# Pairs of inverses moved whole and in place, and one store per segment for rows and left products

## The chip, the cores and the metric

The kernel runs on one core of a Trainium2 chip. The metric is the time of one execution in device microseconds; lower is better. TensorE (PE) multiplies matrices, with weight loads (PEld) beside it; VectorE (DVE), ScalarE (ACT) and GpSimd (POOL) work elementwise; transfers run on 16 DMA engines and are issued from the queues of SP, ACT and POOL. A queue issues in its order: an issue that has to wait holds all behind it.

## What is computed

Two independent halves, laid side by side along the last axis of the output, (1, 2048, 2048) bf16.

```python
def _A_ref(x, mem0, Wq, Wk, Wv, Wo, seg_len):       # x (1, 2048, 1024), 32 heads of 128, seg_len 32
    mem = mem0                                      # (1, 8, 1024)
    for s in range(n_seg):                          # 64 segments, one after the other
        h = jnp.concatenate([mem, xs], axis=1)      # 8 + 32 rows
        q, k, v = (einsum('btd,dhe->bhte', h, W) for W in (Wq, Wk, Wv))
        p = _softmax(where(mask, einsum('bhqe,bhke->bhqk', q, k) * scale, -1e9))
        o = einsum('bhte,hed->btd', einsum('bhqk,bhke->bhqe', p, v), Wo)
        mem = o[:, :M, :].copy()                    # the first 8 rows go on
        outs.append(o[:, M:, :])                    # 32 rows are output

def _B_ref(u, A_re, A_im, B_re, B_im, C_re, C_im, log_dt, Dskip):   # u (1, 2048, 1024)
    K = einsum('dn,dnl,dn->dl', Cc, exp(logdA * l), dB).real
    y = irfft(rfft(u padded) * rfft(K padded))      # a long convolution per channel
    return y + u * Dskip
```

## The kernel before

**Three stages.** First tables are built for the convolution and, in between, everything of the first half that does not depend on the running memory is projected ahead. Of the 40 rows of a segment the last 8 ("left" rows) are such: their keys, queries and values come from DRAM tensors PKd and VXd. Then the transform runs, and then the loop over 64 segments, which ends in one large product for the left rows.

**The transform** (part_b) works in 16 blocks: b // 4 is a quarter of the channels (dq, 256 columns), b % 4 a part of the frequencies. A block multiplies the spectrum of u (read from DRAM by load_u, line 1212) with that of K (pointwise, lines 1377 to 1381 and 1463 on VectorE, L1466 on POOL). While quarter dq is being built, the quarter before it is turned back: two of its eight inverses per block from block 4 on, and the last eight after block 15. An inverse (line 1515) yields 2 x 128 rows of 256 columns: 16 products with MI (L1512), and one with the identity (L1524) that adds u times Dskip; ScalarE scales the sum (L1526) into a tile yb of three buffers, and ACT's queue stores yb one inverse later (L1529). The rows of u come on SP's queue, one transfer of 128 KB per inverse (load_inverse, L1481), three inverses ahead; two neighbours share a tile uu of three buffers, which VectorE multiplies by Dskip (skips, L1489).

SP's queue is written by hand: after these loads, or between them, it issues the segments' weights (load_resident, L268, 512 KB each) as places for them come free. The last eight places are the buffers of MI; they are freed one by one by the last eight inverses, and the weight for each is issued behind the inverse that frees it. K for the second half of the channels is loaded in block 6 (L1095).

**The loop over segments** (part_a). Most weights stay in SBUF. Twelve blocks of 512 KB do not fit and are read again in each segment from DRAM copies WD (stage, L340) into four buffers wst on SP's queue. One block, K7, is held in two PSUM banks and copied in each segment to a scratch area called arena by four copies on VectorE (load_kept and fetch, through words, L335). TensorE's products with them are L414 (q, k, v) and L527 (Wo). The small inputs come on ACT's queue: arena<-PKd (L376), needed first by POOL L428, and arena<-VXd (L382). The segment's result lies in arena as ob: ob[:, 0] holds the 32 rows by 4 quarters of the columns, ob[:, 1] the weighted values of the left rows. Two stores on ACT's queue take them away at the end of the segment:

```python
392:         nc.scalar.dma_start(out=OLd[s // 8][:, 256 * (s % 8):256 * (s % 8) + 256], in_=ob[:, 1, :])
393:         rows = out_a[s * SL:s * SL + SL, :].rearrange("r (q d) -> q r d", q=4)
394:         if s + 1 < NS:
395: 
396:             nc.scalar.dma_start(out=rows, in_=ob[:, 0, :])
```

The next segment writes over ob again with its evicted q (ACT L420) and its softmax (DVE L465), which therefore wait until the stores have landed.

**The end.** In the last segment two of eight pieces of OLd, each of 8 segments, are read back (raw, L576), the other six after it (L652); POOL and VectorE sort them by head (L573); TensorE multiplies them with Wo in four blocks of 64 products (L664), and each block's rows XM to SL of its segments are stored (L670).

The framework puts in all semaphore waits. A transfer also waits until the one eight before it has landed.

Of the kernel before, what the change touches and what calls it, by code (L numbers as in the profile page):

```python
# [10 lines left out]
BF16 = mybir.dt.bfloat16  # L11
# [4 lines left out]
ACT = mybir.ActivationFunctionType  # L16
# [58 lines left out]
class Ahead:  # L75
# [3 lines left out]
    def __init__(self, ctx, tc, x, src, seg_len):  # L79
        self.nc, self.tc, self.x, self.src = tc.nc, tc, x, src  # L80
        self.S, self.Dm = x.shape
        self.SL, self.XM = seg_len, 24
        self.XL, self.KC, self.NS = seg_len - 24, self.Dm // 128, self.S // seg_len
        dram = ctx.enter_context(tc.tile_pool(name="a_dram", bufs=1, space=bass.MemoryType.DRAM))
        self.VXd = dram.tile([self.NS + 1, 128, 256 + self.KC * self.XM], BF16, name="VXd")
        self.PKd = dram.tile([self.NS, 128, 512], BF16, name="PKd")
        self.PVd = [dram.tile([self.NS * self.XL, 2048], BF16, name="PVd%d" % t) for t in range(2)]
        self.OLd = dram.tile([self.NS // 8, 128, 8 * 256], BF16, name="OLd")

    def open(self, ctx):  # L90
        self.pool = ctx.enter_context(self.tc.tile_pool(name="a_pre", bufs=1, side="right"))
# [166 lines left out]


EARLY = (6, 3)  # L260
PAIRS = (0, 4, 2, 6, 8, 12, 10, 14)
LATE = 8


# [7 lines left out]
def part_a(ctx, tc, x, src, WD, HE, seg_len, out_a, ahead, W_res, rest, places, first):  # L272
    nc = tc.nc
    S, Dm = x.shape
    M = 8
    SL = seg_len
    E = 128
    KC = Dm // 128
    NS = S // SL
    assert SL == 32 and M == 8 and Dm == 1024 and HE == 4096  # L280
    XM = 24
# [1 line left out]
    NK = SL + M  # L283
    scale = float(E ** -0.5)

    VXd, PKd, OLd = ahead.VXd, ahead.PKd, ahead.OLd
    ident, mask, BD, BDx, BDL, hT = ahead.consts
    mx, S_ = ahead.low["mx"], ahead.low["S"]

# [53 lines left out]
    def load_kept(key):  # L343
        kept[key] = {}
        for n in (1,) if key in HALF else (0, 1):
            kept[key][n] = ps_k.tile([128, 512], F32, name="keep", tag="keep%d" % sum(len(b) for b in kept.values()))
        if key in HALF:
            w = wst.tile([128, 2048], BF16, name="wst", tag="w%d" % (loads[0] % SLOTS))
            loads[0] += 1
            h_ = ahead.low["half"] if key[0] == "q" else wres.tile([128, 1024], BF16, name="Whalf")  # L350
            for n, t_ in ((1, w[:, 0:1024]), (0, h_[:])):
                nc.sync.dma_start(out=t_, in_=src(key)[:, n, :] if key[0] == "o" else src(key)[:, 1024 * n:1024 * n + 1024])
            words(kept[key][1][:], w[:, 0:1024])
            halves[key] = [(0, 1024, h_)]
# [46 lines left out]
    load_kept(("k", 0, 7))  # L401
    fetch(("k", 0, 7))
    pk = load_pk(0)
    between["q", 0, 2] = lambda: load_kept(("q", 0, 7))
    between["v", 0, 7] = lambda: load_kept(("o", 15))
    for s in range(NS):
        def quads(m, t, kcs, a=None):
            if a is None:
                a = ps.tile([128, 512], F32, name="acc", tag=BANK[m, t])
            for kc in kcs:  # L410
                w = unit((m, t, kc))
                for g in range(4):
                    for o_, rhs in columns(w, 512 * g, 512):
                        nc.tensor.matmul(a[32 * g:32 * g + 32, o_:o_ + rhs.shape[1]], lhsT=hT[:, kc, :], rhs=rhs,  # L414
                                         start=(kc == 0), stop=(kc == KC - 1), tile_position=(0, 32 * g), skip_group_check=True)
            return a

        def evac(a, name):
            q = at(name, 512)
            nc.scalar.copy(out=q, in_=a[:])  # L420
            return q
# [156 lines left out]
        quads("v", 0, range(4, KC), a)  # L578
        scores(1, sc1, QT1, KT1)
# [69 lines left out]
                nc.sync.dma_start(out=wo[u][:].rearrange("e (h d) -> e h d", h=2), in_=src(("o", u)))  # L649
    stores(NS - 1, ob)  # L650
    for j in range(2, 8):
        nc.sync.dma_start(out=raw[j][:], in_=OLd[j])  # L652
# [56 lines left out]
def part_b(ctx, tc, u, A_re, A_im, B_re, B_im, C_re, C_im, log_dt, Dskip, out_b, ahead, copies, residents, first_state):  # L709
# [761 lines left out]
    NIV = 3  # L1471
    unsent, pairs, turn_of = [], [], [0]

    def load_inverse(dq, c):
        r, mc = c // 4, c % 4
        i = turn_of[0] % 2
        turn_of[0] += 1
        if i == 0:
            pairs.append(iv.tile([128, 2, 2, DQ], BF16, name="uu", tag="uu", bufs=3))
        uu = pairs[-1][:, i]  # L1480
        sy.dma_start(out=uu, in_=u_v[r][:, mc:mc + 2, DQ * dq:DQ * dq + DQ])  # L1481
        return uu

    def skips():
        dq = todo[0][0]
        uu = pairs.pop(0)
        d = slice(DQ * dq, DQ * dq + DQ)
        uu = uu[:].rearrange("p i a d -> p (i a) d")
        v.tensor_tensor(out=uu, in0=uu, in1=Dsk[:, d].unsqueeze(1).to_broadcast([128, 4, DQ]), op=ALU.mult)  # L1489

    def inverses(n):

        for _ in range(n):
            dq, c = todo.pop(0)
            inverse(dq, c, nxt.pop(0))
            if len(todo) >= NIV:
                nxt.append(load_inverse(*todo[NIV - 1]))

    early = {}

# [14 lines left out]
    def inverse(dq, c, uu):  # L1515
        r, mc = c // 4, c % 4
        d = slice(DQ * dq, DQ * dq + DQ)
        if (dq, c) in early:
            yp = early[dq, c]
            products_back(yp, dq, c, range(3, 4))  # L1520
        else:
            yp = ps_y.tile([128, 2, DQ], F32, name="yp", tag="yp")[:]
            products_back(yp, dq, c, range(4))
        pe.matmul(yp.rearrange("p b d -> p (b d)"), lhsT=ident[:], rhs=uu.rearrange("p b d -> p (b d)"), start=False, stop=True, skip_group_check=True)  # L1524
        yb = iv.tile([128, 2, DQ], BF16, name="yb", tag="yb", bufs=3)
        sc.activation(out=yb[:], in_=yp, func=ACT.Copy, scale=float(2.0 / PLEN))  # L1526
        while unsent:
            unsent.pop(0)()
        unsent.append(lambda: sc.dma_start(out=out_v[r][:, mc:mc + 2, d], in_=yb[:]))  # L1529

    todo = [(dq, c) for dq in range(4) for c in PAIRS]
    nxt = []
    Bs = [None] * 4
    l4 = k1[0:4, 2560:3072].rearrange("p (r n) -> p r n", r=4)
    w4 = k1[0:4, 3072:4096]
    for b in range(16):
# [3 lines left out]
        points = pointwise(b, now)  # L1540
        next(points)
        if b >= 4:
            skips()
        if 0 < b < 15:
            load_u(b + 1)
        if b == 3:
            v.tensor_scalar(out=ident[:], in0=ident[:], scalar1=float(PLEN / 2), scalar2=None, op0=ALU.mult)
            nxt = [load_inverse(*todo[n_]) for n_ in range(NIV)]
# [41 lines left out]
        if b == 10:  # L1590
            state.send(ps_y.tile([128, 8, 128], BF16, name="yp", tag="yp")[:, :, 0:8])
        if b >= 4:
            inverses(2)
    begun = [ps_h.tile([128, 2, 2, DQ], F32, name="hps", tag="h") for _ in range(2)]
    for n_ in range(3):
        inverse_begin(3, PAIRS[n_], begun[n_ // 2][:, n_ % 2])
    ctx2.close()
    for n_ in range(8):
        if n_ % 2 == 0:
            skips()  # L1600
# [5 lines left out]
    while unsent:  # L1606
        unsent.pop(0)()
    for _ in resident:
        pass

# [157 lines left out]
```

## Time and profile before

| | us |
|---|---|
| median of 3 runs | 1952.72 (1950.53 to 1953.33) |
| the profiled execution | 1947.41 |
| its span | 1945.70 |
| transform's blocks and last inverses, about | 440 to 614 |
| first segment | 614.4 to 648.3 |
| a segment, median of the others | 19.5 |
| left products | 1885.8 to 1941 |

A line of the profile names the line of the code, the engine and the operation, and out<-in by tile names. "PE acc L414 <- DMA wst<-WD_v" is a wait: line 414 on PE could not begin until that transfer landed. In the chain of waits each step is followed back from the end of the program to what released it. A transfer is cut into pieces (packets), each on one of 16 engines; "DMA share" is the busy share of these engines, mean.

### The profile page before, as it was taken

What the parts mean: (1) busy time and instruction counts of PE and PEld (TensorE: products, weight loads), DVE (VectorE), ACT (ScalarE), POOL (GpSimd) and SP (SyncE); (2) the same over time, 40 slices, a digit from 0 to 9 for tenths busy, and PEclk for the clock granted to TensorE, in tenths of its full rate; (3) what the DMA queues carried; (4) which work ended last, traced back from release to release, by engine and by line L of the source; (5) the groups of instructions that cost most, each with busy time, mean ns of one, the idle gap of its engine ahead of it and who ended that gap; (6) DMA issues with size and microseconds to landing.
All of it is one profiled execution on the core that took longest, in us unless ns stands there. A gap on an engine that the chain in (4) does not pass through costs nothing.

```text
span 1945.7 us, 73775 instructions
## 1 busy us (share of the span) xinstructions
PE 1787.6 (92%) x31526; PEld 1092.0 (56%) x31564; DVE 1357.6 (70%) x3362; ACT 918.6 (47%) x1654; POOL 496.5 (26%) x885
## 2 busy tenths in 40 slices
PE   8999999887886899999999999999999999999998
PEld 3666665555763455555555555555555555555554
DVE  8599989888992666666666767666766666666650
ACT  8799989850012344344444444444444443434430
POOL 2354545336552111111111212121112111111130
PEclk9999999878988999999999999999999999999999
DMA  7889898867689999999999999999999999999991
GB/s 216 244 236 273 240 279 240 235 194 248 189 280 306 357 341 354 327 343 343 338 346 351 335 348 348 342 353 339 351 344 340 339 350 336 343 335 338 344 354 32
DMA packets 337341, 591.06 MB, mean 304 GB/s; under 512 B 94848, under 2 KB 211048, under 8 KB 334964
## 3 DMA queue, kind: packets, MB, share of 16 engines
q1 hardware_dynamic: 284824, 531.85, 79.8%
q10 hardware_dynamic: 45532, 29.57, 4.9%
q0 software_dynamic: 6656, 24.92, 3.4%
q8 instruction: 247, 4.05, 0.8%
q14 instruction: 82, 0.67, 0.1%
HBM read 528.78 MB, written 68.47 MB: 307 GB/s over the span
## 4 chain that ended last, share of the span: by engine, by line
PE 45%; DMA 32%; DVE 13%; ACT 6%; issue 3%; POOL 1%; SPq 0%; ACTq 0%; DVEq 0%; POOLq 0%
PE acc L414 20%; DMA wst<-WD_v 11%; DMA wst<-WD_o 9%; PE pp L527 7%; DMA wst<-WD_k 3%; PE pe L664 3%; DMA arena<-PKd 3%; PE tr L425 2%; PE pro L184 2%; DMA out_dram<-arena 2%; PE pro L197 1%; DMA uu<-in_B_u_dram 1%; DVE nr L1266 1%; DMA out_dram<-yb 1%; DMA wst<-WD_q 1%
## 5 line engine op out<-in xcount | busy, mean ns | idle before, releaser
L414 PEld LDWEIGHTS <-a_hT 128*32 128x32 bf16 x12352 | 326.9, 96 | 324.8 <-issue 70.0
L420 ACT CAST arena<-acc 128x512 bf16<-128x512 f32 x384 | 224.7, 585 | 395.0 <-PE acc L414 315.3
L527 PEld LDWEIGHTS <-arena 128*32 128x32 bf16 x8256 | 215.2, 96 | 78.0 <-issue 54.2
L414 PE MATMUL acc<-wst,a_hT 128*32 128x512 bf16 x2304 | 229.7, 382 | 31.4 <-DMA wst<-WD_v 24.1
L428 POOL COPY arena<-arena 128x128 bf16<-128x128 bf16 x128 | 37.4, 292 | 703.7 <-PE tr L425 362.0
L335 DVE TENSOR_SCALAR arena<-keep 128x256 int32<-128x256 int32 (+1 forms) x512 | 175.4, 394 | 28.0 <-PE acc L414 27.9
L414 PE MATMUL acc<-XM,a_hT 128*32 128x512 bf16 x2560 | 173.0, 381 | 0.0
L454 DVE TENSOR_REDUCE a_mx<-sc 128x4 f32<-128x160 f32 (+1 forms) x192 | 71.6, 373 | 79.4 <-PE sc L442 78.0
L197 PE MATMUL pro<-XM,wsl 128*128 128x512 bf16 x480 | 119.5, 387 | 4.7 <-DVE kst L206 1.5
L527 PE MATMUL pp<-W_o,arena 128*32 128x256 bf16 x3584 | 121.5, 273 | 1.4 <-issue 1.4
L414 PE MATMUL acc<-W,a_hT 128*32 128x512 bf16 x1536 | 119.4, 382 | 0.5 <-issue 0.5
L542 DVE COPY arena<-tr 128x512 bf16<-128x512 bf16 x64 | 27.2, 424 | 124.7 <-PE tr L425 124.7
L458 ACT ACTIVATE sc<-sc 128x160 f32<-128x160 f32 (+1 forms) x192 | 63.9, 333 | 104.9 <-DVE sc L455 104.0
L462 DVE TENSOR_REDUCE a_mx<-sc 128x4 f32<-128x160 f32 (+1 forms) x192 | 72.7, 379 | 55.2 <-ACT sc L458 55.0
L489 POOL TENSOR_TENSOR arena<-arena,a_BD 128x128 bf16<-128x128 bf16 x128 | 51.0, 399 | 218.7 <-DVE arena L472 211.5
L1266 DVE TENSOR_SCALAR nr<-ptt 128x456 f32<-128x456 int16 x128 | 80.2, 626 | 31.3 <-PE ptt L1244 28.5
L1258 ACT ACTIVATE E<-pa 128x648 bf16<-128x648 f32 x128 | 87.6, 711 | 17.9 <-PE pa L1250 15.9
L527 PE MATMUL pp<-wst,arena 128*32 128x256 bf16 x1536 | 76.1, 274 | 18.2 <-DMA wst<-WD_o 15.3
L414 PE MATMUL acc<-wq,a_hT 128*32 128x512 bf16 x1024 | 92.5, 383 | 0.0
L425 PEld LDWEIGHTS <-arena 128*128 128x128 bf16 x1024 | 57.9, 98 | 59.6 <-ACT arena L420 28.6
L513 ACT CAST arena<-pv 128x512 bf16<-128x512 f32 (+1 forms) x128 | 61.3, 479 | 63.4 <-PE pv L499 36.4
L414 PE MATMUL acc<-g,a_hT 128*32 128x512 bf16 x1024 | 91.0, 380 | 0.0
(342 smaller groups left out, 3963.2 us busy)
## 6 DMA issues: line engine op xcount, KB each, us to landing
wst<-WD_v SPq DMA_DIRECT2D x256, 512.0 KB
wst<-WD_k SPq DMA_DIRECT2D x192, 512.0 KB
wst<-WD_o SPq DMA_DIRECT2D x192, 512.0 KB
wst<-WD_q SPq DMA_DIRECT2D x128, 512.0 KB
Ud<-ux POOLq DMA_DIRECT2D x16, 1024.0 KB, 7.8
wq<-Ud SPq DMA_DIRECT2D x32, 512.0 KB
wsl<-in_A_Wk_dram SPq DMA_DIRECT2D x16, 512.0 KB
wsl<-in_A_Wv_dram SPq DMA_DIRECT2D x16, 512.0 KB
```

The source lines that it names most:

```text
L197: nc.tensor.matmul(a[:], lhsT=w[:, kc, 128 * j:128 * j + 128], rhs=xTl[:, kc, :, :].rearrange("p s k -> p (s k)"), start=(kc == 0), stop=( ...
L335: nc.vector.tensor_scalar(out=out.bitcast(I32), in0=in_.bitcast(I32), scalar1=0, scalar2=None, op0=ALU.bitwise_or)
L414: nc.tensor.matmul(a[32 * g:32 * g + 32, o_:o_ + rhs.shape[1]], lhsT=hT[:, kc, :], rhs=rhs, start=(kc == 0), stop=(kc == KC - 1), tile_pos ...
L420: nc.scalar.copy(out=q, in_=a[:])
L425: nc.tensor.transpose(out=p[:, hl, :, :].rearrange("p a b -> p (a b)"), in_=q[:, 128 * hl:128 * hl + 128], identity=ident[:])
L454: nc.vector.tensor_reduce(out=m_, in_=x, axis=AX.X, op=ALU.max)
L458: nc.scalar.activation(out=flat(sc, i), in_=flat(sc, i), func=ACT.Exp, scale=scale)
L462: nc.vector.tensor_reduce(out=m_, in_=x, axis=AX.X, op=ALU.add)
L513: copy(out=o[:, i:i + n], in_=p[:, i:i + n, :].rearrange("p a (g q) -> p a g q", g=4))
L527: nc.tensor.matmul(po[32 * qt:32 * qt + 32, o_:o_ + rhs.shape[1]], lhsT=oT[:, h % 4, (h % 16) // 4, :], rhs=rhs, start=False, stop=(h == 3 ...
L1258: sc.activation(out=T["E", r, e // 4][:, lo:lo + 8 * NE].rearrange("p (i c) -> p i c", i=2), in_=T.pop(("p", r, e))[:, :, 0:4 * NE], func= ...
L1266: v.tensor_scalar(out=T["n", r, e // 4][:, lo:lo + 8 * NT], in0=T.pop(("t", r, e))[:, 0:8 * NT].bitcast(I16)[:, 0:16 * NT:2], scalar1=floa ...
```

## The change

- *Pairs.* The inverses are taken in the order 0, 2, 4, ... (PAIRS), so that two neighbours cover the four row groups of one residue r. A pair's rows of u are loaded in one transfer of 256 KB (load_pair), two blocks ahead and in front of that block's weights, and its results are stored in one.
- *In place.* ScalarE writes each result over the rows of u that it used; yb is gone, uu has four buffers, and the last pair has a pool of its own.
- *Order at the end.* The last two pairs are loaded ahead of the seven weights that need no place of MI, and these are issued before the last eight inverses instead of behind the first of them. K is loaded in block 5.
- *First segment.* It reads K7 from the tile it was loaded to; K7 goes to PSUM only after the first k.
- *Loop.* ob is stored whole, 1 KB per partition, to a DRAM tensor RSd. The left products are read back from it in pieces of 512 B (load_raw). The rows of all segments are copied from RSd to the output, DRAM to DRAM, by four transfers on SP's queue after the loop (rows_out).

```diff
-        self.OLd = dram.tile([self.NS // 8, 128, 8 * 256], BF16, name="OLd")
+        self.RSd = dram.tile([self.NS, 128, 512], BF16, name="RSd")
...
-PAIRS = (0, 4, 2, 6, 8, 12, 10, 14)
+PAIRS = (0, 2, 4, 6, 8, 10, 12, 14)
...
     def stores(s, ob):
-        nc.scalar.dma_start(out=OLd[s // 8][:, 256 * (s % 8):256 * (s % 8) + 256], in_=ob[:, 1, :])
-        rows = out_a[s * SL:s * SL + SL, :].rearrange("r (q d) -> q r d", q=4)
-        if s + 1 < NS:
-
-            nc.scalar.dma_start(out=rows, in_=ob[:, 0, :])
-        else:
-            for q in range(4):
-                nc.scalar.dma_start(out=rows[q][0:XM], in_=ob[32 * q:32 * q + XM, 0, :])
-
-    load_kept(("k", 0, 7))
-    fetch(("k", 0, 7))
+        nc.scalar.dma_start(out=RSd[s], in_=ob.rearrange("p a b -> p (a b)"))
+
+    def load_raw(j):
+        nc.sync.dma_start(out=raw[j][:].rearrange("p (s f) -> p s f", s=8), in_=RSd[8 * j:8 * j + 8, :, 256:512].rearrange("s p f -> p s f"))
+
+    def rows_out():
+        rows = out_a.rearrange("(s r) d -> s r d", r=SL)
+        for q in range(4):
+            nc.sync.dma_start(out=rows[:, 0:XM, 256 * q:256 * q + 256], in_=RSd[:, 32 * q:32 * q + XM, 0:256])
+
+    ahead_of["k", 0, 7] = [(0, 2048, first["k", 0, 7])]
...
         k0 = evac(a, "k0")
+        if s == 0:
+            load_kept(("k", 0, 7))
...
     for j in range(2, 8):
-        nc.sync.dma_start(out=raw[j][:], in_=OLd[j])
+        load_raw(j)
+    rows_out()
...
+    def load_pair(n_, pool, bufs=4):
+        uu = held[n_] = pool.tile([128, 2, 2, DQ], BF16, name="uu", tag="uu", bufs=bufs)
+        sy.dma_start(out=uu[:].rearrange("p i a d -> p (i a) d"), in_=rows_of(u_v, n_))
...
+    def inverses(n_, i):
+        while ended:
+            ended.pop(0)()
+        inverse(n_ // 4, PAIRS[2 * n_ % 8 + i], held[n_][:, i])
+        if i:
+            ended.append(lambda: sc.dma_start(out=rows_of(out_v, n_), in_=held[n_][:].rearrange("p i a d -> p (i a) d")))
...
-        yb = iv.tile([128, 2, DQ], BF16, name="yb", tag="yb", bufs=3)
-        sc.activation(out=yb[:], in_=yp, func=ACT.Copy, scale=float(2.0 / PLEN))
...
+        sc.activation(out=uu, in_=yp, func=ACT.Copy, scale=float(2.0 / PLEN))
...
         if 0 < b < 15:
             load_u(b + 1)
+        if b >= 4:
+            load_pair(b - 2, iv)
...
-        if b == 6:
+        if b == 5:
             ks.append(load_k(1, k1[:, 0:2560], 0))
...
     ctx2.close()
+    last = ctx.enter_context(tc.tile_pool(name="b_last", bufs=1))
+    load_pair(14, iv)
+    load_pair(15, last, 1)
+    for _ in range(7):
+        next(resident)
     for n_ in range(8):
         if n_ % 2 == 0:
-            skips()
-        inverses(1)
+            skips(12 + n_ // 2)
+        inverses(12 + n_ // 2, n_ % 2)
         if n_ == 1:
             next(state)
-        for _ in range(9 if n_ == 0 else 1):
-            next(resident, None)
-    while unsent:
-        unsent.pop(0)()
+        next(resident)
+    while ended:
+        ended.pop(0)()
```

More of the change, by code (lines that the diff above doesn't have):

```diff
@@ L284, in part_a @@
     scale = float(E ** -0.5)
-    VXd, PKd, OLd = ahead.VXd, ahead.PKd, ahead.OLd
+    VXd, PKd, RSd = ahead.VXd, ahead.PKd, ahead.RSd
     ident, mask, BD, BDx, BDL, hT = ahead.consts
@@ L651, in part_a @@
     for j in range(2, 8):
-        nc.sync.dma_start(out=raw[j][:], in_=OLd[j])
+        load_raw(j)
+    rows_out()
     for j in range(2, 8):
@@ L1469, in pointwise, with rows_of, skips @@
         eng.tensor_tensor(out=to[:, 2:0:-1], in0=odd[:, 0], in1=odd[:, 1, ::-1], op=ALU.subtract)
[L1471 to L1497, printed above, removed]
+    held, ended = {}, []
+    def rows_of(t_, n_):
+        return t_[n_ % 4][:, :, DQ * (n_ // 4):DQ * (n_ // 4) + DQ]
+    def load_pair(n_, pool, bufs=4):
+        uu = held[n_] = pool.tile([128, 2, 2, DQ], BF16, name="uu", tag="uu", bufs=bufs)
+        sy.dma_start(out=uu[:].rearrange("p i a d -> p (i a) d"), in_=rows_of(u_v, n_))
+    def skips(n_):
+        d = slice(DQ * (n_ // 4), DQ * (n_ // 4) + DQ)
+        uu = held[n_][:].rearrange("p i a d -> p (i a) d")
+        v.tensor_tensor(out=uu, in0=uu, in1=Dsk[:, d].unsqueeze(1).to_broadcast([128, 4, DQ]), op=ALU.mult)
+    def inverses(n_, i):
[4 more added lines that the diff above has]
+            ended.append(lambda: sc.dma_start(out=rows_of(out_v, n_), in_=held[n_][:].rearrange("p i a d -> p (i a) d")))
     early = {}
@@ L1524, in inverse @@
         pe.matmul(yp.rearrange("p b d -> p (b d)"), lhsT=ident[:], rhs=uu.rearrange("p b d -> p (b d)"), start=False, stop=True, skip_group_check=True)
-        yb = iv.tile([128, 2, DQ], BF16, name="yb", tag="yb", bufs=3)
-        sc.activation(out=yb[:], in_=yp, func=ACT.Copy, scale=float(2.0 / PLEN))
-        while unsent:
-            unsent.pop(0)()
-        unsent.append(lambda: sc.dma_start(out=out_v[r][:, mc:mc + 2, d], in_=yb[:]))
-    todo = [(dq, c) for dq in range(4) for c in PAIRS]
-    nxt = []
+        sc.activation(out=uu, in_=yp, func=ACT.Copy, scale=float(2.0 / PLEN))
     Bs = [None] * 4
@@ L1542, in part_b @@
         if b >= 4:
-            skips()
+            skips(b - 4)
         if 0 < b < 15:
             load_u(b + 1)
+        if b >= 4:
+            load_pair(b - 2, iv)
         if b == 3:
             v.tensor_scalar(out=ident[:], in0=ident[:], scalar1=float(PLEN / 2), scalar2=None, op0=ALU.mult)
-            nxt = [load_inverse(*todo[n_]) for n_ in range(NIV)]
+            load_pair(0, iv)
+            load_pair(1, iv)
             ctx_p.close()
@@ L1592, in part_b @@
         if b >= 4:
-            inverses(2)
+            for i in range(2):
+                inverses(b - 4, i)
     begun = [ps_h.tile([128, 2, 2, DQ], F32, name="hps", tag="h") for _ in range(2)]
@@ L1597, in part_b @@
     ctx2.close()
+    last = ctx.enter_context(tc.tile_pool(name="b_last", bufs=1))
[3 more added lines that the diff above has]
+        next(resident)
     for n_ in range(8):
         if n_ % 2 == 0:
-            skips()
-        inverses(1)
+            skips(12 + n_ // 2)
+        inverses(12 + n_ // 2, n_ % 2)
         if n_ == 1:
             next(state)
-        for _ in range(9 if n_ == 0 else 1):
-            next(resident, None)
-    while unsent:
-        unsent.pop(0)()
+        next(resident)
+    while ended:
+        ended.pop(0)()
     for _ in resident:
```

## The prediction

> **What bounds the kernel now.** I read the page's chain first: which work ends last, by line.
>
> ```profile
> PE 45%; DMA 32%; DVE 13%; ACT 6%; issue 3%; POOL 1%; SPq 0%; ACTq 0%; DVEq 0%; POOLq 0%
> PE acc L414 20%; DMA wst<-WD_v 11%; DMA wst<-WD_o 9%; PE pp L527 7%; DMA wst<-WD_k 3%; PE pe L664 3%; DMA arena<-PKd 3%; PE tr L425 2%; PE pro L184 2%; DMA out_dram<-arena 2%; PE pro L197 1%; DMA uu<-in_B_u_dram 1%; DVE nr L1266 1%; DMA out_dram<-yb 1%; DMA wst<-WD_q 1%
> ```
>
> TensorE and transfers share the end: weights (wst) above all, but also the rows' store (out_dram<-arena, 2% or 39 us) and the transform's u and yb. Next the stages, one row each: length, busy time (instructions) of PE, PEld, DVE, ACT, POOL, granted clock, DMA share, GB/s.
>
> ```profile
> 440.00:614.00 174.00, 136.53 (x1088) 106.47 (x1085) 134.69 (x127) 19.10 (x32) 90.79 (x104) 0.90 0.77 248
> 614.00:648.00 34.00, 22.21 (x371) 11.87 (x371) 14.95 (x43) 8.68 (x16) 2.80 (x8) 0.80 0.98 352
> 648.00:1886.00 1238.00, 1169.27 (x25269) 692.41 (x25267) 819.07 (x2584) 515.99 (x1135) 214.39 (x507) 1.00 0.95 343
> 1886.00:1946.00 60.00, 54.71 (x250) 24.75 (x253) 6.04 (x10) 2.80 (x7) 7.47 (x6) 1.00 0.27 90
> ```
>
> The transform's end (440 to 614) has nothing full: no engine is above 79%, DMA 77%. The first segment (614 to 648) is full of transfers. The other 63 segments take 19.65 us each, PE 94% and DMA 95% busy: whichever is freed, the other is near. The last stage is TensorE alone. Then the chain through the transform's end, in order of time (start, us, what):
>
> ```profile
> 545.13 9.58 DMA uu<-in_B_u_dram
> ...
> 566.85 9.22 DMA uu<-in_B_u_dram
> ...
> 585.95 9.36 DMA out_dram<-yb
> 595.47 6.23 DMA out_dram<-yb
> 601.72 2.23 DMA uu<-in_B_u_dram
> ```
>
> A 128 KB load of u takes 9 us because three 512 KB weights stand ahead of it in SP's queue, and a result buffer stays taken for 9 us while its store lands. Last, the waits: of the transform's end (first two lines) and of the segments (us in total, times, longest).
>
> ```profile
> DVE uu L1489 <- DMA uu<-in_B_u_dram: 32.5, 7, 18.1
> ACT yb L1526 <- DMA out_dram<-yb: 9.5, 2, 7.4
> ```
>
> ```profile
> PE acc L414 <- DMA wst<-WD_v: 24.1, 29, 5.0
> ACT arena L420 <- DMA out_dram<-arena: 6.3, 3, 2.2
> DVE arena L465 <- DMA out_dram<-arena: 4.1, 3, 1.5
> ```
>
> **Blocks of the transform.** The product with Dskip (L1489) starts at 455.3 (block 4), 469.5, 479.5, 492.9, 502.9, 512.9, 523.0, 533.0 (block 11), 544.3, 554.7, 564.8, 576.1 (block 15). Undisturbed blocks are 10.04 us apart: VectorE's own chain with POOL L1466 in it. The change loads each pair two blocks ahead, in front of that block's weights, and moves the K loads from block 6 to block 5, where SP issued nothing from 471.5 to 477.1. So blocks 4 to 11 can shrink from 77.7 to 7 x 10.04 = 70.3: 7.4 us, of which I take 6.5. What is late next is the spectrum's own load (L1212), issued 7.7 us ahead of its use. A pair's buffer is loaded again two blocks after its use. That load waits on SP, ahead of weights, for a store that is issued about 5 us after the pair's product; SP reaches it 20 us after that product, and the slowest such store in the chain took 9.4 us, so nothing stands still. Where a store took over 15 us, SP would stop with the weights behind it.
>
> **Blocks 11 to 15, the last eight inverses, the first segment.** TensorE's last inverse ends at 613.2. From block 15's product (576.1) its own work is 24 us: 0.8 and 4.3 for that block's two, 4.5 for three begun sums, then eight inverses of 0.5 to 2.3 us. The rest of 37 is waits: 7.4 and 2.1 for yb, 7.1 for u. In place results and early rows remove them, 14 us on TensorE. But weights are the limit there. From 533 to 648.3 the transfer engines were busy 103.6 of 115.3 us (summed packets); the 11.7 idle us are all that can be won however fast the inverses get. 3.6 of them (580 to 585) lie ahead of weights that wait for POOL to let go of a buffer (584.2); that wait stays, though a backlog may fill it. I take 6 of 11.7. The four copies of K7 that the first segment leaves out (L335, 0.3 us each) lie in that same full stage: nothing. Sum: 6.5 + 6 = **-12.5 us**.
>
> **The segments.** Two stores (128 pieces of 512 B each) become one (128 of 1 KB). In ACT's queue such pieces take 27.2 ns and, loaded, 49.0 ns: 256 x 27.2 / 16 = 0.43 us of all 16 engines against 128 x 49.0 / 16 = 0.39. That is the floor: 0.04 x 63 = 2.7 us. The other bound comes from the rows' store alone: its semaphore rises once within 1 us of the issue, before data moves, and then four times as data lands; for every other transfer of the segment it rises 16 times. So its 128 pieces are 32 on each of four engines, 0.87 us, and those four lose 0.87 + 0.22 and gain 0.39: 0.70 us per segment. If they pace every weight, 0.70 x 63 = 44 us. Between 2.7 and 44 I go by the nearest rows: the weights issued just behind this store (second to fourth of V) land after 5.52, 5.73 and 5.80 us, median, those far from it (last of V, first and third of Wo) after 5.42, 5.43 and 5.43. 0.1 to 0.4 us late, with 24.1 / 63 = 0.38 us per segment of PE waiting for V: I take 0.2 x 63 = **-13 us**, the waits on out_dram<-arena (10.4 us) within it. [...]
>
> ACT also issues one store (0.33 us) instead of two (0.33 + 0.55), at a point where it next waits for PE anyway: nothing.
>
> **The end.** The left products are read in 512 B pieces: 1024 x 27.2 / 16 = 1.74 us against 128 x 178.5 / 16 = 1.43 (4 KB pieces in the segments). Two of these loads fall into the full last segment: +0.6. Six follow it; the second block of products needs two of them at 1899.5, and in the trace the copies from them end at 1894.5, so 0.6 more is hidden. Then the rows: 4 x 1536 pieces, 6144 x 27.2 / 16 = 10.4 us (12 at the 30.8 ns that loads of 512 B averaged in the first stage), between about 1900 and 1920, under TensorE and in idle transfer engines. The last store starts at 1941.8. SP's stores of blocks 0 and 1 queue behind them, and nobody waits for those. If this cover were gone it would cost the 10 to 12 us.
>
> **Sum.** -12.5 - 13 + 0.6 = -24.9. The profiled execution took 1947.4 us (span 1945.7), so 1922.5; the median of the three runs, 1952.7, is 5.3 above it, and I predict against that: **1928 us**.
>
> **Rivals.**
> 1. *As forecast*, 1928: 0.50.
> 2. *The segments don't care*: the stores were 2% of the transfers and the weights' window sets the pace. For it: landings behind the store are late by tenths only. Then -12.5 - 2.7 + 0.6: 1938. 0.20.
> 3. *Four engines paced the loop*: -12.5 - 44 + 0.6: 1897. For it: a mean DMA share of 95% with four engines 0.65 us (3%) above the mean would have them at 98 to 99%. Against: PE is at 94%, and becomes the bound at about 18.7 us (the shortest segments now), or 0.9 less per segment. 0.13.
> 4. *Given back*: the transform ends early, but full transfers let the first segment end only 3 us sooner: -3 - 13 + 0.6: 1937. 0.08. That the u loads come late all the same belongs here.
> 5. *Slower*: before, Q's eviction (ACT L420) and the softmax (L465) waited for the rows' store; now they wait for one store that holds both halves. It decides by one point: today the rows' last piece moves 6.9 us, median, after the issue of arena<-PKd, and the eviction is ready 8.7 after it (1010.0 in the segment of 1001.25); in 4 of 62 segments it came at 9.5 to 10.6, and those four lasted 20.6 to 21.0 us instead of 19.5. Should the one store land that late in half of the segments, it costs 31 x 1.25 = 39 us: 1952.7 - 12.5 + 39 = 1979. Against it: one transfer on 16 engines instead of a second one on four. 0.06.
> The remaining 0.03 is no change.
>
> **Range and chances.** About 0.2% (3.9 us) is what a measurement of this kernel can tell from no change. Cases 1, 2, 4 and most of 3 lie below 1948.8: faster 0.90, same 0.04, slower 0.06. The range reaches from near case 3 to the upper edge of case 2: 1903 to 1943.
>
> **What would show it.** Blocks 10 us apart with no wait of L1489 on u; the last result ending near 590; DMA share above 0.85 from 440 on; the first PKd load of the second segment near 635; segments of 19.4 us with less waiting for WD_v and none on the store; the rows' copy done long before the last store. Wrong would be: blocks still 11 us apart, a first segment that ends at 645, segments unchanged (case 2) or near 18.9 (case 3), a wait of L420 on RSd (case 5).

## The result and the profile after

| | before | after |
|---|---|---|
| median, us | 1952.0 (13 runs, 1942.9 to 1956.2) | 1938.05 (13 runs, 1924.4 to 1946.1) |
| after / before | 1 | 0.9935, 95% interval 0.9910 to 0.9959 |
| profiled execution, us (span) | 1947.41 (1945.7) | 1942.13 (1940.4) |
| last result of the transform | 613.25 | 593.26 |
| load of PKd for the second segment (its start) | 648.32 | 635.46 |
| 62 whole segments, mean between PKd loads | 19.61 | 19.70 |
| last PKd load to the end of the last product | 76.9 | 78.5 |

The change gains 14 us by the medians, 12.7 (8 to 17.6) by the ratio. Predicted were 1928 us, 1903 to 1943. The profiled execution of after lies 4 us above its median and that of before 5 below, so the two traces differ by only 5 us; a small difference between two single traces is not to be trusted below some 5 us in the loop (0.08 us per segment).

First the page's chain of after, by engine and by line:

```profile
PE 46%; DMA 33%; DVE 12%; ACT 5%; issue 2%; POOL 1%; ACTq 0%; SPq 0%; POOLq 0%; DVEq 0%
PE acc L414 19%; DMA wst<-WD_v 12%; DMA wst<-WD_o 9%; PE pp L527 8%; DMA arena<-PKd 4%; PE pe L667 3%; DMA wst<-WD_k 3%; DMA wst<-WD_q 2%; PE tr L425 2%; PE pro L184 2%; PE yp L1508 1%; DVE nr L1269 1%; PE hps L1224 1%; PE pro L197 1%; PE pa L1224 1%
```

The entries that the change aimed at are gone from this list: out_dram<-arena (2%), uu (1%), out_dram<-yb (1%). But the share of transfers rose from 32 to 33%: WD_v and arena<-PKd have a per cent more each. The same by stages, with the columns of the stage table of before:

```profile
440.00:596.00 156.00, 133.14 (x1104) 104.75 (x1108) 132.55 (x125) 19.11 (x32) 88.61 (x102) 0.93 0.81 258
596.00:635.00 39.00, 20.02 (x347) 10.80 (x340) 12.32 (x35) 8.61 (x16) 2.81 (x8) 0.69 1.02 374
635.00:1875.00 1240.00, 1165.18 (x25130) 689.97 (x25133) 815.56 (x2571) 514.83 (x1131) 215.39 (x505) 1.00 0.96 342
1875.00:1940.00 65.00, 60.39 (x403) 28.76 (x391) 10.16 (x24) 4.19 (x10) 8.28 (x8) 1.00 0.52 155
```

The transform's end is 18 us shorter (156 against 174) and the first segment 5 us longer (39 against 34) at a DMA share of 1.02. So the inverses are 20 us sooner, the second segment only 12.9. The chain through the first segment of after (start, us, what) shows who took the seven back:

```profile
594.85 8.56 DMA W<-in_A_Wo_dram
603.43 7.11 DMA a_half<-in_A_Wq_dram
...
614.39 5.57 DMA arena<-VXd
620.02 5.45 DMA wst<-WD_v
```

and the waits of TensorE and POOL in all of after (us in total, times, longest):

```profile
POOL arena L428 <- DMA arena<-PKd: 343.8, 51, 8.1
...
PE acc L414 <- DMA wst<-WD_v: 27.1, 31, 4.1
...
PE acc L414 <- DMA a_half<-in_A_Wq_dram: 14.0, 1, 14.0
```

a_half is the loaded half of the q block Q7, which the first segment fetches (load_kept). It is issued at 603.43, behind the first blocks of Wo in SP's queue: the transfer eight before it is the first of them, and that one lands at 603.41. TensorE, done with the inverses at 593.2, works until 596.6 and then waits 14.0 us for a_half (4.5 before, where it was issued 2.4 us after the last inverse). The other two lines are the loop: waiting for V is up from 24.1 to 27.1 us, POOL's for PKd from 278 to 344.

The blocks of the transform did not get to 10.04 us. The product with Dskip (now L1486) starts at 452.7 (block 4), 462.7, 476.2, 489.6, 499.6 and so on to 529.7 (block 11): 77.0 us for seven blocks, 77.7 before. Two blocks took 13.4. VectorE's first instruction of these two, with its idle time and what ended it in brackets, and SP's queue:

```profile
471.71 1.22 DVE L1380 TENSOR_TENSOR z<-wq,hps 128x1024 f32<-128x1024 f32 x1 [3.52 <-DMA wq<-Ud]
...
485.03 1.22 DVE L1380 TENSOR_TENSOR z<-wq,hps 128x1024 f32<-128x1024 f32 x1 [3.44 <-DMA wq<-Ud]
```

```profile
470.84 1.86 SPq L1098 DMA_DIRECT2D k<-Kx  x3
472.88 2.11 SPq L1098 DMA_DIRECT2D k<-Kp  x2
475.10 1.57 SPq L1215 DMA_DIRECT2D wq<-Ud  x2
```

The wait for u is gone; the wait for the spectrum (wq) has taken its place, 3.5 us twice. For block 6 SP stood 8.5 us ahead of the copies Kp<-Kx (L1087) for the first result store, because a transfer waits for the one eight before it (SP's own wait: us in total, times, longest):

```profile
SPq L1087 <- DMA out_dram<-uu: 8.5, 1, 8.5
```

The five K loads, moved here from block 6, then went ahead of the spectrum of block 7. From block 11 to 15 blocks take 10.08 us (10.8 before), and from block 15's product to the last result 23.2 us (37.2 before), with no wait for yb or u.

### The profile page after: what moved, and what is told of

Same layout as the page of the kernel before. It is cut to its first block, busy times and chain, and to the rows that moved or that the text cites. A ratio compares the mean times of both kernels' runs of the same rounds, so it can differ in the third digit from the quotient of the medians.

```text
span 1940.4 us, 73670 instructions
## 1 busy us (share of the span) xinstructions
PE 1783.4 (92%) x31563; PEld 1091.3 (56%) x31563; DVE 1356.6 (70%) x3357; ACT 918.6 (47%) x1654; POOL 499.4 (26%) x885
## 4 chain that ended last, share of the span: by engine, by line
PE 46%; DMA 33%; DVE 12%; ACT 5%; issue 2%; POOL 1%; ACTq 0%; SPq 0%; POOLq 0%; DVEq 0%
PE acc L414 19%; DMA wst<-WD_v 12%; DMA wst<-WD_o 9%; PE pp L527 8%; DMA arena<-PKd 4%; PE pe L667 3%; DMA wst<-WD_k 3%; DMA wst<-WD_q 2%; PE tr L425 2%; PE pro L184 2%; PE yp L1508 1%; DVE nr L1269 1%; PE hps L1224 1%; PE pro L197 1%; PE pa L1224 1%
## 5 line engine op out<-in xcount | busy, mean ns | idle before, releaser
L414 PE MATMUL acc<-wst,a_hT 128*32 128x512 bf16 x2308 | 230.5, 383 | 36.6 <-DMA wst<-WD_v 27.1
L335 DVE TENSOR_SCALAR arena<-keep 128x256 int32<-128x256 int32 x508 | 174.1, 394 | 26.6 <-PE acc L414 26.6
L544 DVE COPY arena<-tr 128x512 bf16<-128x512 bf16 x64 | 27.2, 424 | 129.2 <-PE tr L425 129.2
L527 PE MATMUL pp<-wst,arena 128*32 128x256 bf16 x1536 | 76.2, 274 | 17.5 <-DMA wst<-WD_o 16.5
L623 ACT CAST arena<-pp 128x128 bf16<-128x128 f32 x64 | 17.0, 265 | 155.7 <-DVE arena L623 155.7
```

What stands on the lines that cost most here:

```text
L335: nc.vector.tensor_scalar(out=out.bitcast(I32), in0=in_.bitcast(I32), scalar1=0, scalar2=None, op0=ALU.bitwise_or)
L527: nc.tensor.matmul(po[32 * qt:32 * qt + 32, o_:o_ + rhs.shape[1]], lhsT=oT[:, h % 4, (h % 16) // 4, :], rhs=rhs, start=False, stop=(h == 3 ...
```

## The experiments

Times are against the kernel before, measured on the same chip. "Second" is the PKd load for the second segment, "segment" the mean of 62 whole segments, both from the one profiled execution of each. The second segment began at 648.3 and 649.3 in the two kernels with the transform of before, and at 632.5 to 637.8, mean 635.7, in five with that of after whose edits lie behind this point; a difference of 2 or 3 us from that mean says nothing. In the two kernels that load PKd early the mark itself stands 1.7 us further ahead.

| kernel | median | ratio (95%) | second | segment |
|---|---|---|---|---|
| after | 1938.05 | 0.9935 (0.9910-0.9959) | 635.5 | 19.70 |
| transform_alone | 1938.28 | 0.9925 (0.9899-0.9951) | 632.5 | 19.59 |
| loop_alone | 1952.60 | 1.0013 (0.9991-1.0034) | 649.3 | 19.60 |
| k_in_block6 | 1937.28 | 0.9939 (0.9918-0.9960) | 637.1 | 19.67 |
| pk_early | 1936.17 | 0.9935 (0.9908-0.9962) | 635.9 | 19.54 |
| both_stalls_pk | 1939.36 | 0.9941 (0.9913-0.9969) | 640.3 | 19.70 |
| rows_more_on_4 | 2047.18 | 1.0498 (1.0447-1.0548) | 637.0 | 21.26 |
| rows_more_on_16 | 1951.26 | 0.9989 (0.9964-1.0014) | 635.6 | 19.61 |
| const_twice_4 | 1960.98 | 1.0035 (1.0005-1.0065) | 637.8 | 19.95 |
| half_weight | 1927.90 | 0.9871 (0.9832-0.9910) | 629.9 | 19.45 |
| rows_behind | 1940.69 | 0.9930 (0.9904-0.9956) | 637.4 | 19.62 |
| own_results | 1942.82 | 0.9933 (0.9911-0.9956) | 639.1 | 19.72 |
| late_weights_out | 1935.57 | 0.9912 (0.9884-0.9941) | 632.4 | 19.72 |

### One part of the change at a time

**transform_alone** is after with the two stores of before (and OLd):

```diff
-        nc.scalar.dma_start(out=RSd[s], in_=ob.rearrange("p a b -> p (a b)"))
+        nc.scalar.dma_start(out=OLd[s // 8][:, 256 * (s % 8):256 * (s % 8) + 256], in_=ob[:, 1, :])
...
+            nc.scalar.dma_start(out=rows, in_=ob[:, 0, :])
```

> The transform's part of the change with the loop of before (two stores per segment, rows of the result on four transfer engines). The change as a whole moved the median by 14 us, where its profiled run shows the second segment beginning 12.9 us sooner and the 62 whole segments taking 5.6 us more in sum. Theory A (the loop's store brings nothing): the whole gain is here, 0.993 of before (-12 to -16 us), and the second segment begins about 635, segments 19.6 us. Theory B (as forecast, half from each part, -12.5 and -13, of which chance hid some): 0.9935 here too, but then the loop alone gains as well, and the sum of both exceeds 14. Theory C (the loop's part gives some of the transform's gain back): more than the whole change, -18 to -20 us, 0.990.

Measured: -14.6 us (-9.6 to -19.7), the whole gain.

**loop_alone** is before with the one store, RSd, load_raw and rows_out of after.

> The loop's part of the change (one store of 128 pieces of 1 KB, rows copied at the end) with the transform of before. Theory A (the segments do not care which store it is): -2 to +1 us, 0.999 to 1.0005; segments 19.6 us; the waits on the store gone from the chain, and arena<-PKd in their place. Theory B (as forecast): -13 us, 0.9935, segments 19.4. Theory C (given back): +4 to +6 us, 1.002 to 1.003, segments 19.7. If four engines paced the loop: -44, 0.978.

Measured: +2.5 us (-1.8 to +6.6), segments 19.60. The forecast of -13 lies outside, and -44 far outside. Its page's chain:

```profile
PE 49%; DMA 31%; DVE 11%; ACT 6%; issue 2%; SPq 0%; POOL 0%; ACTq 0%; DVEq 0%; POOLq 0%
PE acc L415 21%; DMA wst<-WD_v 10%; DMA wst<-WD_o 8%; PE pp L528 8%; DMA wst<-WD_k 4%; PE pe L666 3%; DMA arena<-PKd 3%; DMA wst<-WD_q 2%; PE hps L1223 2%; PE tr L426 2%; PE pro L184 2%; PE yp L1514 2%; DVE nr L1268 1%; DMA uu<-in_B_u_dram 1%; PE pa L1223 1%
```

out_dram<-arena has left the chain, and the segment is as long as it was. The chain of before, asked for the loop, tells what its 2% were (start, us, what):

```profile
784.47 9.89 DMA out_dram<-arena
...
1002.28 9.83 DMA out_dram<-arena
...
1430.25 9.78 DMA out_dram<-arena
```

Three stores of 63 that landed after 9.8 us instead of 5.8, 29.5 us of chain in all (not the 39 of a rounded share), and Q's eviction and the softmax waited 6.3 and 4.1 us for them. transform_alone has the same two stores per segment, none of its row stores took over 7.6 us in the loop, and none lies in its chain. So the entry stood for three late landings of one execution. A chain names the work that ended last, not what its removal is worth: here the next one was ready at nearly the same moment. For transform_alone theory A holds. For loop_alone the segments (19.60, forecast 19.6) are theory A's, but the time, +2.5, lies between A and C and its interval covers both, and arena<-PKd did not take the store's place in the chain (3% as before; TensorE did, 49% against 45%). Of the small loss that theory C expected, the end shows part (below).

### Is it four engines?

Two further stores of the 32 rows per segment, once in the shape with four signals and once over 128 rows; ROWX is scratch.

```diff
         nc.scalar.dma_start(out=RSd[s], in_=ob.rearrange("p a b -> p (a b)"))
+        for i in range(2):
+            nc.scalar.dma_start(out=ROWX[i][...].rearrange("r (q d) -> q r d", q=4), in_=ob[:, 0, :])
```

(rows_more_on_16 has "(r q) d" for "q r d"; const_twice_4 has a resident weight's 256 columns for ob[:, 0, :], so that its scratch holds weights.)

> The changed kernel with two further stores of the 32 result rows per segment (128 pieces of 512 B each, into scratch), in the shape that before had: first dimension 4, so that its semaphore rises four times. Two such stores are 256 x 27.2 ns = 6.96 us of transfer engine time, 0.44 us if spread over 16, 1.74 us if always on the same four. Theory A (a segment lasts as long as the mean load of all engines; the four are not always late, or their lead is taken up by the window of four weights): as the same stores on 16 engines, +20 to +35 us. Theory B (four engines pace every weight): +1.74 x 63 = +110 us, up to 2048. Theory C (stores cost nothing): +5 at most.

> The same two further stores with the same pieces, written as 128 rows, so that all 16 engines take part: 0.44 us of each engine per segment. Theory A (the mean load of the transfer engines sets the segment): +0.44 x 63 = +28 us. Theory B (four engines paced the loop): +28 here, and four times as much in the other kernel. Theory C (TensorE sets the segment): 0 to +5 us.

Measured: +109 us against after in the shape with four signals, +13 (by the ratios +10.5, each with an interval of 5 us to both sides) over 128 rows. The first number is theory B's to the microsecond, and still theory B is wrong. The waits of rows_more_on_4 in the loop (660 to 1855):

```profile
ACT arena L423 <- DMA ROWX<-arena: 94.6, 37, 6.1
...
PE tr L428 <- ACT arena L423: 77.5, 38, 4.8
...
DVE arena L468 <- DMA ROWX<-arena: 54.2, 29, 5.3
```

TensorE waits no longer for weights (for WD_v 11.2 us, 19.9 in after). Q's eviction and the softmax wait for ob, which the late stores still hold (28 of the 37 waits of L423, 74 us, end when an added store lands; the other nine end while ACT still issues the stores. Twelve more waits of L423, 47 us, and 13 of L468, 41 us, which the view puts down to wst<-WD_v, end 0.1 us after an added store lands and belong here too). The first three weights of V land 5.87, 5.83 and 5.98 us after their issue (median; 5.67, 5.69 and 5.83 in after), the two added stores after 6.1 and 8.8; written as 128 rows, the two land after 6.3 and 6.5. To part the two, the same stores from a tile that nobody writes:

> The two further stores on four engines again, with the same pieces and semaphores, but from a weight that is never written over, so that nothing waits for them to land (scratch gets a weight's columns in place of rows). Theory A (the 109 us came from Q's eviction and the softmax waiting for ob until the late stores had landed): no wait on ROWX, +10 to +30 us against the changed kernel, as the same stores on 16 engines gave +13. Theory B (four engines pace the weights): +90 to +110 us again, with waits for WD.

Measured: +23 us against after by the medians, theory A's size. Its waits in the loop:

```profile
PEld L502 <- DMA arena<-VXd: 22.9, 16, 4.3
...
PE pv L502 <- DMA arena<-VXd: 20.2, 16, 4.1
...
PE acc L417 <- DMA wst<-WD_v: 14.9, 29, 1.7
ACT arena L423 <- DMA ROWX<-XM: 14.9, 6, 3.1
```

The last line is no wait for a landing: all six end while ACT still issues the stores. So 86 of the 109 us were the hold on ob. What is left comes through VXd (after has no such waits), the load that stands behind the stores in ACT's own queue: it lands 6.66 us after its issue instead of 5.42, while the weights of V, in SP's queue, land after 5.85, 5.86 and 5.83. So the neighbour in the queue lands 1.2 us later, the loads of the other queue 0 to 0.2; what makes this difference, no run here shows.

### What a transfer microsecond is worth in the loop

```diff
+        if key == ("v", 0, 7):
+            t_ = wst.tile([128, 2048], BF16, name="wst", tag="w%d" % (loads[0] % SLOTS))
+            loads[0] += 1
+            nc.sync.dma_start(out=t_[:, 0:1024], in_=WD[key][:, 0:1024])
+            return [(0, 1024, t_[:, 0:1024]), (1024, 1024, t_[:, 0:1024])]
         return stage(key, WD[key][:])
```

> The changed kernel with one of the twelve streamed weights of a segment (the second of V) read at half its bytes, its first half used twice: that leaves out half of one weight block. 256 KB less of 6.6 MB per segment; 128 pieces of 4 KB (159 to 178 ns) become as many of 2 KB, so 0.6 to 0.75 us of each engine less. Theory A (the mean load of the transfer engines sets the segment): -0.6 to -0.75 us per segment, 19.65 to about 19.0, -38 to -47 us. Theory B (TensorE and the chain through the small loads set it): -5 us at most. In between, the share of the 0.65 us that arrives is the price of a transfer microsecond in this loop.

Measured: -10 us against after by the medians (-12.5 by the ratios, with an interval of 9 to both sides), 5.5 of them already at the start of the second segment. Segments take 19.45 us by the trace, 0.15 to 0.27 less than in the six kernels with the same loop otherwise (19.60 to 19.72), of 0.6 to 0.75 us freed; by the medians it is about 0.1, which their interval does not tell from nothing. Neither theory: by the trace a fifth to two fifths arrive. TensorE is busy 18.5 us in each segment of after (1165.2 / 1240 x 19.70), and its waits for weights in after come to 44 us in all from 650 to 1855 (19.9 + 16.5 + 4.0 + 3.9).

### PKd in the store's place

```diff
         L1 = left_blocks(lt1, 0, "L1")
+        if s + 1 < NS:
+            pk = load_pk(s + 1)
...
-        if s + 1 < NS:
-            pk = load_pk(s + 1)
```

> The changed kernel with the load of PKd issued before the copies of the result instead of between them: as soon as the left blocks of the second half are built, about 1.7 us earlier in each segment. In the changed kernel the chain goes through arena<-PKd with 4% of the span, where before it was 3% and the row store 2%. Theory A (PKd took the place of the store's wait, and where it goes the segment gains part of the 1.7 us): POOL's wait for PKd (344 us) falls by about 100, the wait of the scores for L428 (6.4 us) goes, segments 19.4 to 19.6, -6 to -15 us against the changed kernel, 0.986 to 0.990. Theory B (the weights' transfers pace the segment, whichever load comes last): waits move from PKd to WD, time within 3 us of the changed kernel.

Measured: within 2 us of after. The waits in the loop of pk_early:

```profile
POOL arena L428 <- DMA arena<-PKd: 219.3, 34, 7.7
...
PE sc L439 <- POOL arena L428: 1.4, 4, 0.4
```

They fell as theory A says (338 and 6.4 us in after), and the time hardly did: TensorE waits less for V (12.4 us, 19.9 in after), more for q (6.1, 3.9), and as long for Wo (16.3, 16.5). Theory B, within what is measured: of PKd, store and weights, whichever is moved out of the way, another is due soon after.

### The transform, step by step

**k_in_block6** has the K loads back (`if b == 6`); **both_stalls_pk** has that, PKd early, and all eight Kp copies in block 3.

> The changed kernel with the five K loads back in block 6. In the changed kernel the spectrum loads of blocks 6 and 7 were issued late, and VectorE waited 3.5 us for each: for block 6 behind a transfer of block 4 that waits for the first result store, for block 7 behind the K loads. Expected in the trace: the wait of block 7 gone, that of block 6 still there, blocks 4 to 11 3.5 us shorter, the last result near 590. Theory A (transfers are the limit from 530 on, only idle transfer time counts): the second segment begins at most 1 us sooner, time within 2 us of the changed kernel, 0.993. Theory B (the inverses set the start): 3.5 us sooner, 0.9915.

Measured: block 7 no longer waits, block 6 still does (2.3 us), and now block 8 does: TensorE waits 5.6 us for K itself (L1224, k<-Kx), whose loads are issued from 481 and land at 489 to 492, and VectorE 2.4 us for TensorE. Blocks 4 to 11 take 74.9 us, which is no sign of a gain: with K in block 5 they take 74.0 (transform_alone) to 77.2 us. The last result comes at 594.9, not near 590, and the second segment does not begin sooner (637.1). Theory A, though the 3.5 us that were to test it came only in part.

> The changed kernel with three edits: K loads back in block 6, the second four of the eight Kp copies issued in block 3 and not in block 4 where they waited for the first result store, and PKd loaded early. In the trace neither block 6 nor block 7 should wait for its spectrum (3.5 us each). Theory A (transfers limit the stretch up to the second segment): second segment at 632 to 635, and time as with PKd early alone, 1934 to 1937. Theory B (blocks count): second segment near 629, 1930.

Measured: 1939.4, a miss. The eight Kp copies fill 8 us of SP's queue in block 3, and now the second half of block 5's spectrum is the transfer that has to wait for the first result store (6.8 us):

```profile
469.40 1.22 DVE L1380 TENSOR_TENSOR z<-wq,hps 128x1024 f32<-128x1024 f32 x1 [5.17 <-DMA wq<-Ud]
```

The stall was moved, not removed, and the second segment began at 640.3.

**rows_behind** issues each pair's load behind the block's weights, the last two behind seven weights; **own_results** goes back to three tiles yb and single stores.

```diff
-        if b >= 4:
-            load_pair(b - 2, iv)
...
         for _ in range({1: 2, ...}.get(b, 0)):
             next(resident)
+        if b >= 4:
+            load_pair(b - 2, iv)
```

```diff
-        sc.activation(out=uu, in_=yp, func=ACT.Copy, scale=float(2.0 / PLEN))
+        yb = iv.tile([128, 2, DQ], BF16, name="yb", tag="yb", bufs=3)
+        sc.activation(out=yb[:], in_=yp, func=ACT.Copy, scale=float(2.0 / PLEN))
+        ended.append(lambda: sc.dma_start(out=out_v[r][:, mc:mc + 2, d], in_=yb[:]))
```

> The changed kernel with its pairs and results in place, but each pair's load issued behind that block's weights, and the last two pairs behind seven of the last weights, as before. Theory A (the early rows are what brought the last result 20 us sooner and the second segment 13): VectorE's product waits for u again, last result near 608, second segment 640 to 646, time 0.9955 to 0.999 of before. Theory B (results in place are what counts): second segment near 635, 0.993.

> The changed kernel with pairs loaded early, but results in three tiles of their own and stored one by one, as before (three buffers of pairs, for lack of room). Theory A (early rows count): last result 596 to 600 with waits of ScalarE for out_dram<-yb of 5 to 10 us, second segment 635 to 638, 0.993 to 0.995. Theory B (results in place count): last result near 608, second segment 641 to 646, 0.9955 to 0.999.

Measured: last results at 602.0 and 598.0 (593.3 in after, 613.3 before), second segments at 637.4 and 639.1, times 1940.7 and 1942.8: with the rest of the change, results in place or early rows alone keep most of the gain (theory B of the first, theory A of the second), and which one is worth more is below what was measured. What both kernels have in common (pairs in one transfer of 256 KB, seven weights ahead of the last eight inverses, K7 read from its tile) may have its part in the gain; no kernel here leaves it out. The chain of rows_behind (first fence) and of own_results (second):

```profile
583.32 10.94 DMA uu<-in_B_u_dram
...
602.66 1.30 DVE keep L335 x2
604.37 7.11 DMA a_half<-in_A_Wq_dram
```

```profile
579.78 9.16 DMA out_dram<-yb
...
598.02 7.99 DMA arena<-PKd
606.03 7.10 DMA a_half<-in_A_Wq_dram
```

Each brings back its own wait, u or yb, of 9 to 11 us. But a_half is issued at 604.4 and 606.0 there, and at 603.4 in after. What lets it go differs: in rows_behind the copies of K7 to PSUM (keep) right after the last result, in own_results the load of PKd that is issued right behind the last result and stands eight transfers before a_half, in after a weight of Wo eight before it. When the last result comes sooner, the weights' backlog is next, and 9 or 5 us on TensorE ahead of a_half become at most 2 to 4 behind it.

**late_weights_out** leaves out seven loads of Wo in the first segment:

```diff
-                load_resident(tc, wres, src, k_, W_res)
+                W_res[k_] = W_res[next(k for k in W_res if k[0] == "o")]
```

> The changed kernel without the last seven loads of Wo blocks (512 KB each, issued from 606.7 to 621.3 in the first segment): another Wo block stands in for them, so that part of the second product's weights is wrong. Theory A (from 530 to the second segment transfers are the limit): 7 x 1.45 = 10 us less transfer time, second segment at 624 to 628, 8 to 11 us off the changed kernel, 0.988 to 0.989. Theory B (inverses and the chain of the first segment set it): within 3 us of the changed kernel.

Measured: second segment 632.4, some 3 us sooner and not 8 to 12, time -2.5 against after by the medians, -4.5 by the ratios. Of 10 us of transfers 3 arrive at most; theory A falls as it was put. Its stage row for the first segment shows transfers with room:

```profile
596.00:635.00 39.00, 22.28 (x413) 12.14 (x405) 14.55 (x45) 9.32 (x20) 3.31 (x8) 0.78 0.90 314
```

a_half still comes at 603.6: the seven loads lie behind it. So what binds up to 610 is the order in SP's queue (weights ahead of a_half, and the one eight before it that has to land first), and only behind that, partly, the mass of transfers. Moving a_half ahead of the last Wo blocks was not tried.

No kernel here that does all of the work beats the changed one by more than the measurement tells; transform_alone equals it.

## Why the prediction was right, and where not

The sign, the range and the size of the transform's part were right; the time is that of the second rival ("the segments don't care", 1938, given 0.20), not of the forecast, and lies in the range only because that reached to this rival's upper edge.

- **Blocks 4 to 11, -6.5**: failed. 0.7 us in after, 3.7 in transform_alone (74.0 us), whose transform is the same; 2.8 with the K loads back in block 6. "SP issued nothing from 471.5 to 477.1" was true of before; with the K loads put there, and with a Kp copy that waits for a result store ahead of them, the spectrum became late: the item named as "late next" was late, 3.5 us in two blocks. "Nothing stands still" failed as well: SP stood 8.5 us for the first result store and 7.0 us (587 to 594) for a later one that took 11.4 us to land, each time for the transfer eight before and not for the pair's buffer. The second stop shows no cost, as the transfer engines were busy meanwhile (share 1.04 from 587 to 594). The waits on u went as said.
- **Late transform and first segment, -6**: the mechanism was right, the size too small. TensorE won 20 us up to the last result (14 from block 15 on, as worked out; 2.8 in blocks 11 to 15; block 4 began 2.6 sooner, which varies from 450.9 to 455.8 between kernels). From block 11 to the second segment 105.8 us were needed instead of 115.3: 9.5 of the 11.7 us named as all that can be won. The summed packets fell from 103.6 to 101.0 us for the same 34.7 MB. By the chain, what stopped it was less the sum of bytes than one load's place in a queue; no run moved that load.
- Together -12.9 in the trace and -14.6 in transform_alone for **-12.5**: right in sum by luck, as two errors cancel (0.7 and 9.5 for 6.5 and 6), with the 2.6 of block 4's start on top.
- **Segments, -13**: failed, and it is the miss of the forecast. The step was to read the later landing of three V weights (0.1 to 0.4 us; the first three of four, the prediction says second to fourth) as the work of the row store on four engines. Without that store they land after 5.67, 5.69 and 5.83 us, or 5.52, 5.60 and 5.65 in loop_alone, against 5.52, 5.73 and 5.80: the lateness is not that store's. It may belong to their place in the queue, which no run tested. The weights in flight closest to the store, the last of K just before it and the first of q just behind, landed after 5.99 and 5.82 us before and after 6.08 and 6.06 in after, no sooner. And const_twice_4 shows that even two more stores of that shape move the V weights by 0.2 at most. The "2% or 39 us" of the row store were three late landings, as shown above. The 2.7 us floor was the better end, and even of that only a part can arrive by half_weight's trace.
- **Four engines** (the 44 us, the third rival): the count of four holds, the pace does not. In the trace of before at most four pieces of a row store start within any 23 ns once the store ahead of it has landed (the 36 segments where pieces are then left), and four signals tell of its landing; which engines move them, no run here shows. But with two more stores of that shape in ACT's queue (const_twice_4) the weights in SP's queue land at most 0.2 us later.
- **The slower rival** named a real mechanism: rows_more_on_4 is it, 86 us of late stores that hold ob. The one store of the change lands 6.1 us after its issue (5.9 for the two before), ahead of Q's eviction, so its point was not reached: no wait for the store RSd<-arena appears in after's waits.
- **The end, +0.6**: right sign, 1.6 measured (81.6 and 81.7 us from the last PKd to the end of the span with the old loop, 81.6 to 84.0, mean 83.2, in the seven kernels with the new one and its stores and PKd unaltered). The two early reads of left products are 2048 pieces of 512 B at 27.2 ns, 3.5 us of 16 engines, and the V weight behind them lands after 8.9 and 9.1 us (6.0 and 7.4 with the old loop). The other six and the copy of the rows ended at 1905, under the products, hidden as said.

What stays open: whether the one store costs the segments anything (19.60 to 19.72 in six kernels with it, 19.59 and 19.61 in two without; loop_alone's interval holds both), and how the gain divides between early rows, results in place, and what the two kernels that give up one of them have in common.

## What to carry to other kernels

A transfer on the chain is worth its lead over the next one, not its share: take away one part alone, or look for what else is due at that moment, before a share is turned into microseconds, and count how often it stands there, as three late landings can make 2%. In this loop, with TensorE and transfers both above 90% busy, a freed transfer microsecond brought 0.2 to 0.4 by one kernel's trace. When loads are moved in a hand-written queue, follow each load that is now behind them, and the ones that wait for a store eight transfers back; and ask which single load the next stage waits for, because that one's place decides what an earlier end is worth.

## What the hardware showed that was not expected

Stores with four signals delayed the next load in their own queue (VXd, 5.42 to 6.66 us) far more than the loads in the other queue (0 to 0.2 us). The summed packet time reached 1.04 to 1.06 of the 16 engines' time (600 to 630 in after, at 384 to 403 GB/s), with up to 22 packets under way at once, so the times of packets overlap, and a share of 1 is not the most that a stage can show. The granted clock was 0.50 from 600 to 610, where TensorE did nothing but wait for a_half, and 0.70 and 0.66 in the next two stretches of 10 us, with TensorE busy 8.9 and 5.6 us.
